# Last output tile in three column pieces, and 1/den spread to partitions by DMAs instead of matmuls

## The chip, the cores and the metric

The kernel runs on one core of a Trainium2 chip. The metric is device time in microseconds of one execution. Executions of one kernel mostly scatter by about 0.3 us either way.

## The reference, cut to what matters

```python
def _A_ref(x, wqkv, wo):                       # x: (1, 2048, 640), 32 heads of 20 features
    ...
    pq, pk = phi(q), phi(k)
    kv  = jnp.einsum("bhsd,bhse->bhde", pk, v)
    z   = jnp.einsum("bhsd->bhd", pk)
    num = jnp.einsum("bhqd,bhde->bhqe", pq, kv)
    den = jnp.einsum("bhqd,bhd->bhq", pq, z)[..., None] + 1e-6
    o = num / den
    return o.transpose(0, 2, 1, 3).reshape(B, S, D) @ wo

def _B_ref(x, w1, b1, w2, b2):                 # F = 1536
    return gelu(x @ w1 + b1) @ w2 + b2

return x + _A_ref(xn, ...) + _B_ref(xn, ...)   # xn = layernorm(x)
```

The kernel folds `kv` and `wo` into one matrix `Msb`. An output tile of 128 tokens is then one accumulation: 12 products of the MLP (`HG` with `W2`) and 5 of the attention (`PQ/den` with `Msb`). Dividing by `den` means scaling `PQ`, which has features on its partitions, by a row of 1/den for each head. `rden` has (chunk, head) on its partitions, so each head's row must be spread to the 4 partitions of that head in each of the 5 feature slices.

## The kernel before: the parts that the change touches

Tokens come in 4 chunks of 512 (`CW`), that is 16 tiles of 128. `HW` is 320, `JT` 12, `DT` 5, `H` 32. `E4` is the constant matrix of the matmul that copies each head's row to its partitions. `Pl.ins` records an instruction with the resources it reads and writes, and puts in the waits. Each engine runs its list in the order in which it was recorded.

```python
def rden_step(c, b):                       # spread 1/den of chunk c by a matmul, and scale PQ
    ...
    Pl.ins("tensor", lambda e: e.matmul(bank(b), E4[:, c, :], rden[:], start=True, stop=True), ...)
    Pl.ins("scalar", lambda e: e.activation(rs, bank(b), ACT.Copy), ...)
    for j in range(DT):                    # 5 DVE multiplications of 128x512
        Pl.ins(v, lambda e, j=j: e.tensor_tensor(out=PQ[:, j, cc], in0=PQ[:, j, cc], in1=rs, op=ALU.mult), ...)

def x_again(c):                            # reload of x for the residual, 640 KB, on SyncE
    Pl.ins("sync", ..., writes=[r_xr[c]] + r_xnT, dma=True)

def out_fin(t, b):                         # end of tile t
    s = t % 2                              # two output buffers only
    ...                                    # 10 matmuls PQ*Msb, 320 columns each
    xb(t)
    Pl.ins(v, ... out=halves(out_sb[:, s, :]), in0=pair(b), in1=halves(x_res[:, t, :]) ...)   # eviction
    Pl.ins("sync", lambda e: e.dma_start(ov[t * P:(t + 1) * P, :], out_sb[:, s, :]), ...)     # store

def out_last(t):                           # tile 15: two halves of 320 columns, each evicted and stored
    ...

bs = [out_w2(0)]
db = den_step()                            # den, then 1/den on DVE (rden)
bs += [out_w2(1), out_w2(2, 0, JT // 2)]
rden_step(0, db)
out_w2(2, JT // 2, JT, bs[2])
for t in range(3):
    out_fin(t, bs[t])
for t in range(3, NT - 1):
    b = out_w2(t)                          # 24 matmuls HG*W2
    if t in (3, 6, 10):
        rden_step({3: 1, 6: 2, 10: 3}[t], take(1))
    out_fin(t, b)
out_last(NT - 1)

for (waits, fns, ev, dma) in list(Pl.records["sync"]):   # SyncE waits for all its DMAs at the end
    if dma and ev is not None:
        Pl.wait_event("sync", ev)
```

The eviction of tile 2 writes the same buffer as tile 0, so it waits until the store of tile 0 has landed. The scaling of chunk 1 comes after that eviction in DVE's list.

## Time and profile before

| | before |
|---|---|
| device time, median of 6 runs | 212.06 us (211.77 to 212.39) |
| span in the trace | 210.7 us |
| TensorE busy | 205.5 us, 98% |
| first den matmul's start to last matmul's start | 72.57 us |
| last matmul's start to the end of the span | 3.15 us |

The page of the kernel before, its head (busy us, share of the span, instructions):

```profile
span 210.7 us, 3883 instructions
PE 205.5 (98%) x1585; PEld 140.1 (67%) x1585; DVE 110.5 (52%) x226; ACT 76.8 (36%) x145; POOL 20.5 (10%) x61
```

The chain of waits of the kernel before, in order of time (start us, us, what):

```profile
136.20 5.00 PE ps L600 x36
141.20 0.21 PE ps L570
141.41 8.96 PE ps L600 x66
150.38 0.22 PE ps L570
150.59 13.86 PE ps L600 x102
164.45 0.22 PE ps L570
164.67 18.47 PE ps L600 x136
183.14 0.22 PE ps L570
183.35 24.46 PE ps L600 x180
207.82 0.02 issue
207.84 0.49 DVE out_sb L632
```

L600 is an output matmul and L570 the E4 matmul that spreads 1/den. From 136 us on the chain is TensorE alone, without a gap: each E4 matmul pushes all later work back by 0.22 us. Only the last eviction (L632) and what follows it are not TensorE.

The timeline of the kernel before, 143 to 157 us, all engines, cut to the lines that matter (in brackets: idle before, and what ended it):

```profile
144.44 0.82 DVE L619 TENSOR_TENSOR out_sb<-ps,xnT 128x640 bf16<-128x640 f32 x1 [0.19 <-PE ps L600]
...
145.29 9.41 SPq L622 DMA_DIRECT2D out_dram<-out_sb  x4
...
149.76 0.82 DVE L619 TENSOR_TENSOR out_sb<-ps,xnT 128x640 bf16<-128x640 f32 x1 [2.74 <-DMA out_dram<-out_sb]
...
151.26 1.77 DVE L574 TENSOR_TENSOR PQ<-PQ,ek 128x512 bf16<-128x512 bf16 x5 [0.67 <-ACT ek L572]
...
155.05 1.52 PE L600 MATMUL ps<-Msb,PQ 128*128 128x320 bf16 x10
```

These are the evictions of tiles 0 and 2 (DVE, L619), the first stores on SyncE (SPq), the scaling of chunk 1 and TensorE's first use of it. The eviction of tile 2 already waits for a store (tile 0, issued at 145.29 and landed at 149.64). Nothing is lost by it: TensorE needs the scaled chunk only at 155.05.

SyncE's closing waits in the kernel before (count, ns, first and last start):

```profile
L108 SPq EVENT_SEMAPHORE  x17: 28/28/28, 208.7 to 210.2; - x17
```

The last store landed at 209.94, and the last of these waits ended at 210.23. The waits, not the landing, come last.

### The profile page before, as it was taken

Reading aid. Unit: us, or ns where it says so; the run is one execution under the profiler, and the core shown is the slowest. Engines: PE = TensorE matmul, PEld = TensorE weight load, DVE = VectorE, ACT = ScalarE, POOL = GpSimd, SP = SyncE. Lnnn points to the kernel's source line nnn. Section 1 sums busy time; section 2 is a strip of 40 time slices with the busy share of each in tenths; the row PEclk is TensorE's granted clock in tenths of the full one; section 3 lists DMA queues with packets and bytes.
Section 4 is the critical chain, followed back from the end, with each engine's and each line's share of the span. In section 5 each row is a group of like instructions: output and inputs, shape, how many; then the busy total and the mean of one; then the engine's idle time right before and its main releaser. Section 6 shows DMA issues by size and latency. Waiting matters only on the chain.

```text
span 210.7 us, 3883 instructions
## 1 busy us (share of the span) xinstructions
PE 205.5 (98%) x1585; PEld 140.1 (67%) x1585; DVE 110.5 (52%) x226; ACT 76.8 (36%) x145; POOL 20.5 (10%) x61
## 2 busy tenths in 40 slices
PE   7999999999999999999999999999999999999994
PEld 2689987444457777777666555677777777777772
DVE  4689981000008888999078866468451522263221
ACT  2579887666676554111253575110100100100000
POOL 2244557700000000000000000000000000000000
PEclk9999999999999999999999999999999999999999
DMA  5994758999000000000000000355411010001011
GB/s 165 340 349 99 101 111 101 347 321 346 10 0 0 0 3 0 0 3 0 0 0 3 0 5 0 124 138 170 163 35 54 9 65 31 31 31 34 31 62 33
DMA packets 21787, 17.46 MB, mean 83 GB/s; under 512 B 8713, under 2 KB 21769, under 8 KB 21769
## 3 DMA queue, kind: packets, MB, share of 16 engines
q1 hardware_dynamic: 21088, 16.72, 27.6%
q10 hardware_dynamic: 680, 0.49, 0.9%
q8 instruction: 12, 0.20, 0.4%
q14 instruction: 7, 0.05, 0.1%
HBM read 12.62 MB, written 2.62 MB: 72 GB/s over the span
## 4 chain that ended last, share of the span: by engine, by line
PE 86%; DVE 7%; DMA 4%; SPq 1%; issue 1%; DVEq 0%
PE ps L600 35%; PE ps L356 23%; PE ps L477 10%; PE ps L488 10%; PE ps L510 5%; DMA xPK<-in_A_x_dram 4%; DVE PQ L467 3%; DVE ek L465 1%; DVE W L534 1%; SPq L232 1%; PE ps L530 1%; PE ps L546 1%; DVE ZB L524 1%; PE ps L556 1%; DVE stats L313 0%
## 5 line engine op out<-in xcount | busy, mean ns | idle before, releaser
L600 PE MATMUL ps<-W,HG 128*128 128x320 bf16 x384 | 54.9, 299 | 0.0
L356 PE MATMUL ps<-xnT,W 128*128 128x128 bf16 (+2 forms) x435 | 52.0, 282 | 0.4 <-DMA W<-in_B_w_dram 0.4
L600 PEld LDWEIGHTS ps<-W,HG 128*128 128x128 bf16 x384 | 37.5, 98 | 15.2 <-issue 0.4
L356 PEld LDWEIGHTS ps<-xnT,W 128*128 128x128 bf16 x435 | 35.5, 98 | 16.1 <-DMA W<-in_B_w_dram 0.5
L360 ACT ACTIVATE HG<-ps,b1c 128x128 bf16<-128x128 f32 (+2 forms) x87 | 40.0, 492 | 13.2 <-PE ps L356 11.1
L465 DVE TENSOR_SCALAR ek<-ek 128x512 bf16<-128x512 bf16 (+1 forms) x36 | 10.9, 304 | 40.2 <-ACT ek L464 39.1
L464 ACT ACTIVATE ek<-ps 128x512 bf16<-128x512 f32 (+1 forms) x36 | 23.2, 644 | 20.4 <-PE ps L510 11.2
L619 DVE TENSOR_TENSOR out_sb<-ps,xnT 128x640 bf16<-128x640 f32 x15 | 12.4, 825 | 29.3 <-PE ps L600 26.2
L600 PE MATMUL ps<-Msb,PQ 128*128 128x320 bf16 x160 | 24.2, 299 | 0.0
L510 PE MATMUL ps<-xnT,Wqkv 128*128 128x512 bf16 x100 | 22.1, 379 | 0.0
L477 PE MATMUL ps<-Wqkv,xnT 128*128 128x320 bf16 x160 | 21.9, 299 | 0.0
L488 PE MATMUL ps<-xPK,xn_tm 128*128 128x320 bf16 x160 | 21.9, 299 | 0.0
L572 ACT ACTIVATE ek<-ps 128x512 bf16<-128x512 f32 x4 | 2.4, 597 | 49.2 <-PE ps L570 49.2
L600 PEld LDWEIGHTS ps<-Msb,PQ 128*128 128x128 bf16 x160 | 15.6, 98 | 6.3
L477 PEld LDWEIGHTS ps<-Wqkv,xnT 128*128 128x128 bf16 x160 | 15.7, 98 | 6.2
L488 PEld LDWEIGHTS ps<-xPK,xn_tm 128*128 128x128 bf16 x160 | 15.7, 98 | 6.1
L510 PEld LDWEIGHTS ps<-xnT,Wqkv 128*128 128x128 bf16 x100 | 11.6, 118 | 9.5 <-issue 0.2
L313 DVE BATCH_NORM_STATS2 stats<-xPK 128x6 f32<-128x320 bf16 x32 | 15.2, 475 | 3.5 <-DMA xPK<-in_A_x_dram 2.9
L467 DVE SCALAR_TENSOR_TENSOR PQ<-ps,ek 128x512 bf16<-128x512 f32 x20 | 13.8, 692 | 2.1
L467 DVE SCALAR_TENSOR_TENSOR xPK<-ps,ek 128x640 bf16<-128x640 f32 x16 | 13.2, 825 | 1.7
L498 DVE TENSOR_TENSOR Msb<-Msb,xPK 128x640 f32<-128x640 f32 x14 | 11.6, 825 | 0.5
L574 DVE TENSOR_TENSOR PQ<-PQ,ek 128x512 bf16<-128x512 bf16 x20 | 7.1, 419 | 9.0 <-ACT ek L572 9.0
(64 smaller groups left out, 89.3 us busy)
## 6 DMA issues: line engine op xcount, KB each, us to landing
xnT<-in_A_x_dram SPq DMA_DIRECT2D x4, 640.0 KB, 4.1
Wqkv<-in_A_wqkv_dram SPq DMA_DIRECT2D x3, 800.0 KB, 6.9
out_dram<-out_sb SPq DMA_DIRECT2D x15, 160.0 KB, 1.8
W<-in_B_w_dram SPq DMA_DIRECT2D x1, 1920.0 KB, 15.3
W<-in_B_w_dram SPq DMA_DIRECT2D x3, 480.0 KB, 7.6
xPK<-in_A_x_dram SPq DMA_DIRECT2D x2, 640.0 KB, 9.3
Wo<-in_A_wo_dram SPq DMA_DIRECT2D x1, 800.0 KB, 10.5
xPK<-in_A_x_dram SPq DMA_DIRECT2D x4, 160.0 KB, 4.5
```

What stands on the lines that cost most here:

```text
L313: Pl.ins(v, lambda e: e.bn_stats(stats[:, s, 6 * h:6 * h + 6], x_in[:, t, h * HW:(h + 1) * HW]), reads=[r_x[t]], writes=[r_stats[s]])
L356: Pl.ins("tensor", [(lambda e, k=k: e.matmul(bank(b, 0, w), W1[:, k, jb * P:(jb + 1) * P], xnT[:, k, tok], start=(k == 0), stop=(k == DT - ...
L360: Pl.ins("scalar", lambda e: e.activation(HG[:, jb, tok], bank(b, 0, w), ACT.Gelu_apprx_tanh, bias=b1c[:, jb:jb + 1]), reads=[B_[b], r_b1c ...
L464: Pl.ins("scalar", lambda e: e.activation(e2, src, ACT.Exp), reads=br, writes=[r_ek[s]])
L465: Pl.ins(v, lambda e: e.tensor_scalar(et, et, 1.0, 1e-6, ALU.min, ALU.add), reads=[r_ek[s]], writes=[r_ek[s]])
L467: Pl.ins(v, lambda e: e.scalar_tensor_tensor(out=d2, in0=src, scalar=0.0, in1=e2, op0=ALU.max, op1=ALU.add), reads=br + [r_ek[s]], writes= ...
L477: fns.append(lambda e, k=k, h=h, b=b, t=t: e.matmul(bank(b + h, 0, HW), xnT[:, k, t * P:(t + 1) * P], Wqkv[:, k, D + h * HW:D + (h + 1) * ...
L488: Pl.ins("tensor", [(lambda e, t=t, h=h, b=b, f=f: e.matmul(bank(b + h, 0, HW), xn_tm[:, t, f * P:(f + 1) * P], PK[:, t, h * HW:(h + 1) * ...
L498: Pl.ins(v, lambda e, t=t: e.tensor_tensor(out=zsum, in0=zsum, in1=PK[:, t, :], op=ALU.add), reads=[r_PK[t], r_zsum], writes=[r_zsum])
L510: Pl.ins("tensor", [(lambda e, k=k, j=j, b=b: e.matmul(bank(b), Wqkv[:, k, j:D:DT], xnT[:, k, cc], start=(k == 0), stop=(k == DT - 1))) fo ...
L600: return lambda e: e.matmul(bank(b + h, 0, HW), l, r[:, h * HW:(h + 1) * HW], start=(i == 0), stop=(i == JT + DT - 1))
L619: Pl.ins(v, lambda e: e.tensor_tensor(out=halves(out_sb[:, s, :]), in0=pair(b), in1=halves(x_res[:, t, :]), op=ALU.add), reads=B_[b:b + 2] ...
```

## The change

The intent is twofold. First, the last tile should end with a smaller piece, so that less eviction and store follow the last matmul. Second, three of the four E4 matmuls on the busy TensorE should be replaced by DMAs, on engines that are nearly idle.

```diff
+        def rden_dma(c):
+            for i in range(4):
+                Pl.ins("sync", lambda e, i=i: e.dma_start(rdb(c)[i:P:4, :], rden[H * c:H * (c + 1), :]),
+                       reads=[r_rden], writes=[r_rdb[c][i]] + ([r_rdb[0][i]] if c == 3 else []), dma=True)
...
         def out_last(t):
-            b = take(2)
             xb(t)
-            for h in range(2):
-                hs = slice(h * HW, (h + 1) * HW)
...
+            lo = 0
+            for i, w in enumerate((HW, 3 * 64, P)):
+                b = take(1)
...
         rden_step(0, db)
         out_w2(2, JT // 2, JT, bs[2])
+        for c in range(1, NC):
+            rden_dma(c)
         for t in range(3):
             out_fin(t, bs[t])
         for t in range(3, NT - 1):
             b = out_w2(t)
             if t in (3, 6, 10):
-                rden_step({3: 1, 6: 2, 10: 3}[t], take(1))
+                rden_scale({3: 1, 6: 2, 10: 3}[t])
             out_fin(t, b)
         out_last(NT - 1)
```

`rden_scale(c)` is the five DVE multiplications alone. Chunk 0 keeps its E4 matmul. The twelve DMAs stand on SyncE, ahead of the store of tile 0.

More of the change, by code (lines that the diff above doesn't have):

```diff
@@ L564, in den_step, with rden_scale, rdb @@
             return b
+        def rden_scale(c):
+            cc = slice(c * CW, (c + 1) * CW)
+            for j in range(DT):
+                Pl.ins(v, lambda e, j=j: e.tensor_tensor(out=PQ[:, j, cc], in0=PQ[:, j, cc], in1=rdb(c), op=ALU.mult),
+                       reads=r_rdb[c] + [r_PQ[c][j]], writes=[r_PQ[c][j]])
+        ekf = ek[:].rearrange("p a d -> p (a d)")
+        r_rdb = [[R_("rdb%d_%d" % (c, i)) for i in range(4)] for c in range(NC)]
+        def rdb(c):
+            return ekf[:, c % 3 * CW:(c % 3 + 1) * CW]
         def rden_step(c, b):
-            cc = slice(c * CW, (c + 1) * CW)
-            s = c % 3
-            rs = ek[:, s, 0:CW]
             Pl.ins("tensor", lambda e: e.matmul(bank(b), E4[:, c, :], rden[:], start=True, stop=True),
                    reads=[r_E4, r_rden], writes=[B_[b]])
-            Pl.ins("scalar", lambda e: e.activation(rs, bank(b), ACT.Copy), reads=[B_[b]], writes=[r_ek[s]])
-            for j in range(DT):
-                Pl.ins(v, lambda e, j=j: e.tensor_tensor(out=PQ[:, j, cc], in0=PQ[:, j, cc], in1=rs, op=ALU.mult),
-                       reads=[r_ek[s], r_PQ[c][j]], writes=[r_PQ[c][j]])
+            Pl.ins("scalar", lambda e: e.activation(rdb(c), bank(b), ACT.Copy), reads=[B_[b]],
+                   writes=r_rdb[c] + r_ek)
+            rden_scale(c)
+        def rden_dma(c):
+            for i in range(4):
+                Pl.ins("sync", lambda e, i=i: e.dma_start(rdb(c)[i:P:4, :], rden[H * c:H * (c + 1), :]),
+                       reads=[r_rden], writes=[r_rdb[c][i]] + ([r_rdb[0][i]] if c == 3 else []), dma=True)
         def x_again(c):
@@ L594, in bass_parallel_sum__linear_attn_block__dense_activation_gelu__prompt_kernel, with mm_ops @@
             x_again(c)
+        r_out3 = R_("out3")
+        def mm_ops(t, i):
+            tok = slice(t * P, (t + 1) * P)
+            return ((HG[:, i, tok], W2[:, i, :]) if i < JT else (PQ[:, i - JT, tok], Msb[:, i - JT, :]))
         def mm(b, t, i, h):
-            tok = slice(t * P, (t + 1) * P)
-            l, r = ((HG[:, i, tok], W2[:, i, :]) if i < JT else (PQ[:, i - JT, tok], Msb[:, i - JT, :]))
+            l, r = mm_ops(t, i)
             return lambda e: e.matmul(bank(b + h, 0, HW), l, r[:, h * HW:(h + 1) * HW],
@@ L625, in out_last @@
         def out_last(t):
-            b = take(2)
             xb(t)
-            for h in range(2):
-                hs = slice(h * HW, (h + 1) * HW)
-                Pl.ins("tensor", [mm(b, t, i, h) for i in range(JT + DT)],
-                       reads=[r for i in range(JT + DT) for r in mm_reads(t, i)], writes=[B_[b + h]])
-                Pl.ins(v, lambda e, h=h, hs=hs: e.tensor_tensor(
-                    out=out_sb[:, h, 0:HW], in0=bank(b + h, 0, HW), in1=x_res[:, t, hs], op=ALU.add),
-                    reads=[B_[b + h], r_xb[t]], writes=[r_out[h]])
-                Pl.ins("sync", lambda e, h=h, hs=hs: e.dma_start(ov[t * P:(t + 1) * P, hs], out_sb[:, h, 0:HW]),
-                       reads=[r_out[h]], dma=True)
+            lo = 0
+            for i, w in enumerate((HW, 3 * 64, P)):
+                b = take(1)
+                o = out_sb[:, (0, 1, 0)[i], (0, 0, HW)[i]:(0, 0, HW)[i] + w]
+                hs = slice(lo, lo + w)
+                lo += w
+                fns = []
+                for q in range(JT + DT):
+                    l, r = mm_ops(t, q)
+                    fns.append(lambda e, l=l, r=r, q=q, b=b, hs=hs, w=w: e.matmul(
+                        bank(b, 0, w), l, r[:, hs], start=(q == 0), stop=(q == JT + DT - 1)))
+                Pl.ins("tensor", fns, reads=[r for q in range(JT + DT) for r in mm_reads(t, q)], writes=[B_[b]])
+                Pl.ins(v, lambda e, b=b, hs=hs, w=w, o=o: e.tensor_tensor(
+                    out=o, in0=bank(b, 0, w), in1=x_res[:, t, hs], op=ALU.add),
+                    reads=[B_[b], r_xb[t]], writes=[r_out3 if i == 2 else r_out[i]])
+                Pl.ins("sync", lambda e, hs=hs, o=o: e.dma_start(ov[t * P:(t + 1) * P, hs], o),
+                       reads=[r_out3 if i == 2 else r_out[i]], dma=True)
         bs = [out_w2(0)]
```

## The prediction

> **What bounds the kernel now.** TensorE. Section 1 of the page: PE busy 205.5 of 210.7 us, clock 1.00. The chain of waits, in order of time, is unbroken PE work from 124.9 us to 207.8, then one DVE eviction (0.49). PE waits for nothing in the output stage. The median is 212.05 us.
>
> **Removed.** Three E4 matmuls of 512 columns (chunks 1 to 3). Each holds the chain for 0.22 us (pieces of the chain at 150.4, 164.5, 183.1), so 0.65 us in sum, all on the critical path. Three ACT copies of 0.60 us go too off the path; the DVE scalings (5 x 0.42 us a chunk) stay.
>
> **Last tile.** The second half, 17 matmuls of 320, becomes 17 of 192 and 17 of 128. The trace shows starts of 55.8 ns at 128 columns, 109.2 at 256, 135.8 at 320 and 215.8 at 512, each with its own weight load. That is the Trainium skill's N/2.4+2.5 (TensorE: Matmul & The Clock Gate, Back-to-back issue gap); the ~81 ns that the section gives for 128 columns beside weight loads does not show here. Estimate for 192: 82.5 ns. 17 x (82.5+55.8) = 2.35 us against 2.31: +0.04. The eviction on the chain shrinks: 320 columns 0.492, 640 columns 0.825, hence about 0.29 for 128: -0.20. The last store is issued 0.16 us earlier. The middle piece's eviction fits under the last 0.95 us of matmuls.
>
> **The end.** After the last store is issued (208.36, done 208.69), SyncE runs 17 semaphore waits, two semaphores each, from 208.74 to 210.23, about 0.065 us apart, with one hole of 0.48. The last store landed at 209.94, before these waits were through: the end is set by the waits, not by the landing. The change adds 12 DMAs in the spread and one more store, 13 more semaphores, so about 7 more waits: +0.42 us.
>
> **The spread.** The 12 DMAs (32 KB each, SBUF to SBUF) are issued on SyncE behind the x reload, whose fourth issue is at 144.36, and ahead of the first output store (now 145.29). Back-to-back issues took 0.40 to 0.55 us early in the trace, so about 5.5 us: the first store moves to about 150 and lands near 152. DVE's eviction of tile 2 waits for that (now it starts at 149.76), and chunk 1's scaling follows, 152.9 to 154.6. PE needs its first part at about 154.8 and the rest 0.27 us apart. Slack near 1.2 us: no stall expected, but it is the weak point[...]. Chunks 2 and 3 have ample time.
>
> **Sum.** 212.05 - 0.65 - 0.16 + 0.42 = 211.66; with some weight on a small PE stall, 211.7 us. Range 211.2 to 212.2. Faster by over 2%: 0.01; within 2%: 0.98; slower: 0.01.
>
> **What would show it.** Right: the chain of waits without E4 pieces; PE ending about 0.6 us earlier; starts of 82 and 56 ns in the last tile; last eviction near 0.29 us; about 24 closing waits on SyncE, taking near 1.9 us, ending after the last landing; DVE's idle before tile 2's eviction longer by 2 us, with no idle PE near 155. Wrong: PE idle between 150 and 156 with DVE scaling or a DMA as releaser; a last landing that ends after the waits.
>
> **What would make it wrong.** Longer issue of the 12 DMAs, stalling PE (+0.5 to 2 us); closing waits that cost less, or a second hole of 0.5; stores of 256-byte rows landing slowly.

## More of the kernel before

All runs used here are with a granted TensorE clock of 0.99 to 1.00.

The argument uses two things: ratios from interleaved runs, and distances in time inside the traces.

Absolute times of two traces should not be subtracted from one another.

## The result, and the profile after

The kernel after the change takes 212.36 us (median of 6 runs, 212.14 to 212.84) against 212.06 before. The ratio is 1.0017, with a 95% interval of 1.0003 to 1.0031. Here and below a ratio is the mean time of one kernel's fast runs over that of the other's in the same rounds, so it is not quite the ratio of the medians. The change makes the kernel about 0.3 us slower, where 0.35 us of gain was predicted.

| | before | after |
|---|---|---|
| first den matmul's start to last matmul's start | 72.57 us | 73.27 us |
| last matmul's start to the end of the span | 3.15 us | 2.82 us |
| store of tile 0 issued, landed | 145.29, 149.64 | 151.80, 153.84 |

The page after, its head:

```profile
span 210.4 us, 3928 instructions
PE 204.4 (97%) x1592; PEld 140.3 (67%) x1599; DVE 110.3 (52%) x227; ACT 75.1 (36%) x142; POOL 20.5 (10%) x61
```

The chain of waits after, in order of time:

```profile
155.12 0.01 DVE PQ L569
155.13 0.05 issue
155.18 47.97 PE ps L618 x350
203.15 4.67 PE ps L654 x51
207.83 0.02 issue
207.85 0.29 DVE out_sb L657
```

The E4 pieces are gone (the profile did not trace the chain back past 155 us), but at 155.12 there is something new. TensorE is no longer the head of its own chain: it was released by DVE's scaling of PQ (L569). At the end, the last eviction has shrunk from 0.49 to 0.29 us, as intended.

The timeline after, 143 to 157 us, all engines, cut to the lines that matter:

```profile
144.12 7.64 SPq L587 DMA_DIRECT2D ek<-rden  x12
...
151.80 3.35 SPq L640 DMA_DIRECT2D out_dram<-out_sb  x3
153.97 0.82 DVE L637 TENSOR_TENSOR out_sb<-ps,xnT 128x640 bf16<-128x640 f32 x1 [7.56 <-DMA out_dram<-out_sb]
154.71 1.76 DVE L569 TENSOR_TENSOR PQ<-PQ,ek 128x512 bf16<-128x512 bf16 x5
155.18 0.11 PEld L618 LDWEIGHTS ps<-Msb,PQ 128*128 128x128 bf16 x2 [1.13 <-DVE PQ L569]
155.18 1.79 PE L618 MATMUL ps<-Msb,PQ 128*128 128x320 bf16 x10 [0.80 <-DVE PQ L569]
155.51 0.11 PEld L618 LDWEIGHTS ps<-Msb,PQ 128*128 128x128 bf16 x2 [0.22 <-DVE PQ L569]
```

Read it from top to bottom. SyncE issues the twelve spread DMAs from 144.12 to 151.76, and only then the store of tile 0. That store lands at 153.84. The eviction of tile 2, which reuses the buffer, sat idle 7.56 us for it. The scaling of chunk 1 stands behind that eviction in DVE's list. TensorE, which would have been ready at about 154.2, waits for the scaling, and then follows it slice by slice: its 10 matmuls take 1.79 us in place of 1.52. Nothing in the chain waits for the DMAs' data: the rows for chunk 1 had landed by 149.06.

What the twelve DMAs cost SyncE (ns least/median/most, first and last start), and its closing waits, after:

```profile
L587 SPq DMA_DIRECT2D ek<-rden x12: 470/594/602, 144.1 to 151.2; - x12
```

```profile
L108 SPq EVENT_SEMAPHORE  x24: 17/28/28, 208.6 to 209.9; - x24
```

A median of 594 ns each, and about 0.64 us from one issue to the next. The 24 closing waits took no longer than the 17 before: the hole of 0.48 us does not appear among them.

### The profile page after: what moved, and what is told of

Its sections match the earlier page's. It is cut to its first block, busy times and chain, and to the rows that moved or that the text cites. A ratio compares the mean times of both kernels' runs of the same rounds, so it can differ in the third digit from the quotient of the medians.

```text
span 210.4 us, 3928 instructions
## 1 busy us (share of the span) xinstructions
PE 204.4 (97%) x1592; PEld 140.3 (67%) x1599; DVE 110.3 (52%) x227; ACT 75.1 (36%) x142; POOL 20.5 (10%) x61
## 5 line engine op out<-in xcount | busy, mean ns | idle before, releaser
L618 PE MATMUL ps<-W,HG 128*128 128x320 bf16 x360 | 51.4, 299 | 0.1
L618 PEld LDWEIGHTS ps<-W,HG 128*128 128x128 bf16 x360 | 35.1, 98 | 14.2 <-issue 0.4
L618 PE MATMUL ps<-Msb,PQ 128*128 128x320 bf16 x150 | 22.8, 299 | 0.8 <-DVE PQ L569 0.8
L510 PE MATMUL ps<-xnT,Wqkv 128*128 128x512 bf16 x97 | 21.4, 379 | 0.3 <-issue 0.2
L618 PEld LDWEIGHTS ps<-Msb,PQ 128*128 128x128 bf16 x150 | 14.2, 98 | 7.4 <-DVE PQ L569 2.0
L492 ACT ACTIVATE W<-ps 128x640 bf16<-128x640 f32 x5 | 3.5, 704 | 18.2 <-PE ps L488 14.6
L322 POOL TENSOR_TENSOR rstd<-veps,mhalf 128x1 f32<-128x1 f32 x16 | 9.2, 575 | 1.3
```

The lines of the kernel that those rows point to most:

```text
L510: Pl.ins("tensor", [(lambda e, k=k, j=j, b=b: e.matmul(bank(b), Wqkv[:, k, j:D:DT], xnT[:, k, cc], start=(k == 0), stop=(k == DT - 1))) fo ...
L618: return lambda e: e.matmul(bank(b + h, 0, HW), l, r[:, h * HW:(h + 1) * HW], start=(i == 0), stop=(i == JT + DT - 1))
```

## The experiments

All gave the right result, and each is compared with runs of the kernel before on the same chip (their medians: 212.13 us beside e1 to e4, 211.90 beside e5, e6, e7 and e9, 212.05 beside e10 and e11). "Stage" below is the time from the first den matmul's start to the last matmul's start in the trace, "end" that from there to the end of the span. The theory at the outset was the reading just given. The rivals were that the tail pieces cost the time, that the bytes of the spread come late or crowd the DMA engines, and that DVE simply has too little time there.

| run | median us | ratio to before (95%) | stage | end |
|---|---|---|---|---|
| before | 212.06 | 1 | 72.57 | 3.15 |
| the change | 212.36 | 1.0017 (1.0003 to 1.0031) | 73.27 | 2.82 |
| e1_tail_only | 211.95 | 0.9997 (0.9984 to 1.0010) | 72.69 | 2.91 |
| e2_spread_only | 212.81 | 1.0053 (1.0025 to 1.0081) | 73.16 | 3.04 |
| e3_scale_early | 211.36 | 0.9965 (0.9953 to 0.9977) | 72.04 | 2.81 |
| e4_act_queue | 211.23 | 0.9958 (0.9946 to 0.9970) | 72.04 | 2.91 |
| e5_three_dmas | 210.91 | 0.9949 (0.9934 to 0.9964) | 72.04 | 2.53 |
| e9_chunk3_later | 211.47 | 0.9980 (0.9955 to 1.0006) | 72.04 | 2.80 |
| e6_trim_before | 211.68 | 0.9980 (0.9967 to 0.9994) | 72.57 | 3.13 |
| e7_more_waits | 214.36 | 1.0111 (1.0093 to 1.0129) | 72.57 | 5.35 |
| e10_early_few_waits | 211.07 | 0.9947 (0.9935 to 0.9958) | 72.04 | 2.53 |
| e11_three_dmas_few_waits | 210.91 | 0.9946 (0.9932 to 0.9960) | 72.04 | 2.50 |

### e1_tail_only: the three pieces without the spread

The new `out_last` is put into the kernel before; the E4 matmuls stay.

> The kernel before with only the last tile in pieces of 320, 192 and 128; E4 matmuls kept. My theory (the tail pieces are a small gain, the loss is in the spread): last store issued about 0.2 us earlier, one closing wait more at most; 211.9 us beside 212.06, that is -0.05 to -0.4 us, no idle PE near 155 us. Rival (small pieces and 256-byte rows are what costs): 212.4 us or more, with the last landing later than 1.6 us after its issue.

The median is 211.95 us and the ratio 0.9997, not to be told from no change by time alone. The trace shows the expected small gain: the end shrinks by 0.24 us, while the stage grows by 0.12 (the last, shorter matmul starts later). There is no idle TensorE near 155 us, and the store of 256-byte rows landed 1.44 us after its issue, faster than the 1.58 of the 320-column store. The rival that the tail costs the time is out.

### e2_spread_only: the spread without the three pieces

The change with `out_last` of the kernel before.

> The change with the last tile of the kernel before. My theory: three E4 matmuls less (-0.65), a PE stall of about 1.2 us at tile 3's PQ matmuls near 155 us (+1.2), so 212.6 us. Rival (the tail pieces are what costs): -0.65 alone, 211.4 us.

It took 212.81 us, 0.2 above the expectation; two of its six runs, at 213.89 and 214.66 (the latter at a clock of 0.991), widen the interval, but all of it lies above 1. The loss is in the spread. The timeline of DVE in this kernel, 143 to 157 us:

```profile
154.66 0.82 DVE L637 TENSOR_TENSOR out_sb<-ps,xnT 128x640 bf16<-128x640 f32 x1 [7.58 <-DMA out_dram<-out_sb]
155.40 1.75 DVE L569 TENSOR_TENSOR PQ<-PQ,ek 128x512 bf16<-128x512 bf16 x5
```

It is the same wait of 7.6 us as in the change, and the same late scaling. The stage is 73.16 us; without three E4 matmuls it should be 72.57 - 0.65 = 71.92, so the stall costs 1.24 us.

### e3_scale_early: the scaling ahead of the eviction

```diff
         for t in range(3):
+            if t == 2:
+                rden_scale(1)
             out_fin(t, bs[t])
...
-            if t in (3, 6, 10):
-                rden_scale({3: 1, 6: 2, 10: 3}[t])
+            if t in (6, 10):
+                rden_scale({6: 2, 10: 3}[t])
```

> The change with chunk 1's scaling ahead of tile 2's eviction in DVE's order; the 12 DMAs and the late first store stay as they are. My theory (DVE's eviction of tile 2, waiting for the late first store, holds up the scaling that PE needs): scaling starts near 149 us, when its four DMAs have landed, tile 2's eviction still waits until about 154, PE stall gone, 211.2 us. Rival (the rows of 1/den themselves come late, or DVE is simply short of time there): the stall stays, 212.3 us.

The timeline of DVE, 143 to 157 us, in e3:

```profile
149.23 1.77 DVE L569 TENSOR_TENSOR PQ<-PQ,ek 128x512 bf16<-128x512 bf16 x5 [2.88 <-DMA ek<-rden]
150.91 0.48 DVE L596 TENSOR_TENSOR xnT<-xnT,b2bc 128x640 bf16<-128x640 bf16 x1
154.24 0.82 DVE L637 TENSOR_TENSOR out_sb<-ps,xnT 128x640 bf16<-128x640 f32 x1 [2.85 <-DMA out_dram<-out_sb]
```

The scaling starts at 149.23, as soon as the rows have landed, and is done by 151. Tile 2's eviction still waits until 154.24, as late as before, and it harms nothing. The stage drops from 73.27 to 72.04, by 1.23 us, and the ratio from 1.0017 to 0.9965. The twelve DMAs are all there, issued from 144.40 to 152.03 (144.12 to 151.76 in the change). So neither their data nor DVE's load held TensorE up; the order in DVE's list did, together with the late store. This is the strongest of the tests, because it changes the place of five instructions and nothing else. The time came 0.16 us above the expectation.

### e4_act_queue: the same DMAs from another queue

```diff
-                Pl.ins("sync", lambda e, i=i: e.dma_start(rdb(c)[i:P:4, :], rden[H * c:H * (c + 1), :]),
+                Pl.ins("scalar", lambda e, i=i: e.dma_start(rdb(c)[i:P:4, :], rden[H * c:H * (c + 1), :]),
```

> The change with the 12 DMAs issued by ACT instead of SyncE, same bytes; SyncE then also has 12 semaphores fewer to wait for at the end. My theory (what costs is SyncE's time to issue, 0.64 us each, ahead of the first store): first store issued near 145 us, tile 2's eviction near 150, no stall, about 210.9 us (0.25 of it from the closing waits). Rival (the 12 DMAs load the DMA engines or their descriptor generation, whoever issues them): the first store lands as late as in the change, the stall stays, 212.1 us.

The timeline of DVE, 143 to 157 us, in e4:

```profile
149.19 0.82 DVE L637 TENSOR_TENSOR out_sb<-ps,xnT 128x640 bf16<-128x640 f32 x1 [2.56 <-DMA out_dram<-out_sb]
149.93 1.76 DVE L569 TENSOR_TENSOR PQ<-PQ,ek 128x512 bf16<-128x512 bf16 x5
```

SyncE issued the first store at 144.89, it landed at 149.07, and the stall is gone although the same bytes move: the stage is 72.04. ACT could start the twelve 3 us sooner than SyncE in the change (141.06), as it has no reload of `x` ahead of them, so the bytes move somewhat earlier. Eight of the twelve still landed between 148.18 and 150.35, around the first store, which took 4.17 us to land where it took 4.35 in the kernel before. The rival that the DMA engines are crowded is out. ACT's issues took as long as SyncE's did (about 0.62 us each), but nothing that TensorE needs waits behind them on ACT. The expected 0.25 us from shorter closing waits did not come: 18 waits, but with the hole of 0.48 us among them again.

### e5_three_dmas: one DMA for each chunk

```diff
-            for i in range(4):
-                Pl.ins("sync", lambda e, i=i: e.dma_start(rdb(c)[i:P:4, :], rden[H * c:H * (c + 1), :]),
-                       reads=[r_rden], writes=[r_rdb[c][i]] + ([r_rdb[0][i]] if c == 3 else []), dma=True)
+            src = rden[H * c:H * (c + 1), :].unsqueeze(1).to_broadcast([H, 4, CW])
+            Pl.ins("sync", lambda e: e.dma_start(rdb(c), src),
+                   reads=[r_rden], writes=r_rdb[c] + (r_rdb[0] if c == 3 else []), dma=True)
```

> The change with each chunk's spread as one DMA of 128 rows (every source row read four times) instead of four of 32: 3 DMAs for 12, same bytes, still on SyncE ahead of the first store. My theory (SyncE pays 0.64 us for each DMA back to back, whatever its rows): about 1.9 us in all, first store near 146.5, no stall, and 9 semaphores fewer to wait for at the end; 211.1 us. Rival (the cost goes with rows or bytes, so one such DMA takes about 2.5 us): first store near 151, stall stays, 212.2 us.

What these DMAs cost SyncE in e5 (ns least/median/most, first and last start), and its DVE timeline, 143 to 157 us:

```profile
L587 SPq DMA_DIRECT2D ek<-rden x3: 544/593/674, 144.3 to 145.9; - x3
```

```profile
150.34 0.82 DVE L637 TENSOR_TENSOR out_sb<-ps,xnT 128x640 bf16<-128x640 f32 x1 [3.76 <-DMA out_dram<-out_sb]
151.08 1.75 DVE L569 TENSOR_TENSOR PQ<-PQ,ek 128x512 bf16<-128x512 bf16 x5
```

A DMA of 128 rows and 128 KB costs SyncE 593 ns, the same as one of 32 rows and 32 KB (594). Between these two shapes the cost is per DMA, not per row or byte. Three of them take 2.1 us, the first store is issued at 146.45, and the stall is gone. With nine semaphores fewer at the end, and no hole, the end is 2.53 us. At 210.91 us against 211.90 for the runs of the kernel before beside it, this beats both kernels.

### e9_chunk3_later: eight DMAs ahead of the store instead of twelve

```diff
-        for c in range(1, NC):
-            rden_dma(c)
+        rden_dma(1)
+        rden_dma(2)
         for t in range(3):
             out_fin(t, bs[t])
+        rden_dma(3)
```

> The change with chunk 3's four DMAs issued after the stores of tiles 0 to 2, so 8 of the 12 stand ahead of the first store. My theory: the first store moves up by 4 x 0.64 = 2.5 us to near 149.3, lands near 151.5, scaling of chunk 1 done its first part by 152.7, ahead of PE's need near 154.2: stall gone, 211.3 us. Rival (a DMA of the spread is slow whatever stands behind it): stall stays, 212.3 us.

The first store was issued at 149.89 and landed at 151.93. The timelines of DVE and then of TensorE in e9, 143 to 157 us:

```profile
152.06 0.82 DVE L637 TENSOR_TENSOR out_sb<-ps,xnT 128x640 bf16<-128x640 f32 x1 [4.97 <-DMA out_dram<-out_sb]
152.80 1.75 DVE L569 TENSOR_TENSOR PQ<-PQ,ek 128x512 bf16<-128x512 bf16 x5
```

```profile
151.64 3.42 PE L618 MATMUL ps<-W,HG 128*128 128x320 bf16 x24
154.90 1.52 PE L618 MATMUL ps<-Msb,PQ 128*128 128x320 bf16 x10
```

The scaling starts 2.1 us before TensorE's first use of it, and the 10 matmuls take their normal 1.52 us. The stall is a matter of threshold: four DMAs fewer in the way and it is nil. By time the run is less clear. One of its six executions took 213.05 us, at the lowest clock of the six (0.992, the others 1.00), and pulls the ratio to 0.998, with an interval that touches 1; the median of 211.47 and the stage of 72.04 agree with e3.

### e6_trim_before and e7_more_waits: the closing waits of the kernel before

e6 waits at the end for the last four stores alone. e7 appends 34 more semaphores, all of DMAs already waited for.

```diff
-        for (waits, fns, ev, dma) in list(Pl.records["sync"]):
-            if dma and ev is not None:
-                Pl.wait_event("sync", ev)
+        ends = [ev for (waits, fns, ev, dma) in Pl.records["sync"] if dma and ev is not None][-4:]
+        for ev in ends:
+            Pl.wait_event("sync", ev)
```

```diff
                 Pl.wait_event("sync", ev)
+        Pl.records["sync"].append(([("dma%d" % i, 16) for i in range(34)], [], None, False))
```

> The kernel before with closing waits on its last four stores alone (all other DMAs have been waited for by their users). My theory (the end is set by 17 closing waits, which finish 0.29 us after the last landing): two waits, the last ending about 0.1 us after the last landing, -0.2 us or a little more, 211.85 us. Rival (the landing of the last store sets the end): no change, 212.06 us.

> The kernel before with 34 more semaphores in the closing waits, all long passed: 17 more wait instructions. My theory (each such instruction costs 0.062 us at the end, as in the traces): +1.05 us, 213.1 us. Rival (they run in the shadow of the last landing): +0.75 us or less, or none.

SyncE's closing waits in e6, and in e7 (count, ns least/median/most, first and last start):

```profile
L108 SPq EVENT_SEMAPHORE  x2: 17/22/28, 208.4 to 209.7; - x2
```

```profile
L108 SPq EVENT_SEMAPHORE  x34: 28/28/1219, 208.4 to 212.0; - x34
```

e6 is inconclusive. Its waits did end 0.05 us after the last landing (209.64), yet its end is 3.13 us, no shorter than before. A gap of 0.45 us now lies between SyncE's last two instructions of the closing barrier, behind the waits; the other engines had passed that barrier by 210.04, SyncE only at 210.32. The measured ratio of 0.998 is a small gain that its trace does not account for.

e7 missed. It cost 2.4 us, not 1.05. In its trace the wait for the last store's semaphore was placed first (208.35, lasting 1.22 us until the landing), so the 33 others ran after the landing and none in its shadow. The cost of one is confirmed all the same: after the hole, 29 steps took 212.013 - 210.221 us, 0.062 us each.

The hole has a fixed place in SyncE's list: in all five traces that show it, it stands between the 79th and the 80th instruction that the trace records for SyncE. So it follows the fourth instruction after the last DMA in the kernel before and in e7; the third in e1 and e4, which have one more store ahead of it; and in e6 the fourth too, which is there the closing barrier's drain. In the change, e2, e3, e9 and e10, with 12 more DMAs on SyncE, and in e5 and e11 with 3 more, the 80th comes before the last store is issued, and no such hole appears after it. It is SyncE's, it goes with the count of instructions, and it costs time only where it falls after the last store. What makes it is not shown (the last point of this document says what is known).

### e10_early_few_waits and e11_three_dmas_few_waits

e3 and e5, each with closing waits on its last five stores alone. Here no hole was expected behind the landing.

> e3_scale_early with closing waits on the last five stores alone (the others have been waited for by their users). There 24 waits ended 0.32 us after the last landing, and no hole of 0.48 us stood in SyncE's stream near the end. My theory (closing waits at 0.062 us each delay the end where they outlast the landing): the last wait ends within 0.1 us of the last landing, so from the last matmul's start to the end 2.55 us instead of 2.81; about 0.25 us less than e3, 211.1 us. Rival (the landing sets the end, the waits run in its shadow): 2.8 us as in e3.

> e5_three_dmas with closing waits on the last five stores alone: the candidate for the best version. In e5 the waits ended 0.07 us after the last landing, so both theories expect next to nothing: 2.5 us from the last matmul's start to the end, 210.9 us. If the hole of 0.48 us in SyncE's stream falls behind the landing here, up to 0.45 us more.

SyncE's closing waits in e3, and in e10:

```profile
L108 SPq EVENT_SEMAPHORE  x24: 17/28/28, 207.7 to 209.1; - x24
```

```profile
L108 SPq EVENT_SEMAPHORE  x2: 28/28/28, 208.0 to 208.8; - x2
```

In e10 the end is 2.53 us against 2.81 in e3, as expected (2.55), and its median is 211.07 us. In the absence of the hole the closing waits are a real cost of 0.28 us. In e11 the end is 2.50 against 2.53 in e5, and the time 210.91 us, the same as e5: there was nothing left to take. e5, e10 and e11 are level at ratios of 0.9946 to 0.9949.

## Why the prediction was wrong

- **What bounds the kernel, and the E4 matmuls: right.** The three removed matmuls were priced at 0.65 us. From the stages, e1 to e3 is 72.69 - 72.04 = 0.65 us.
- **The last tile: right.** Predicted starts of 82 and 56 ns; in the trace after they are 82 to 83 and 55 to 56. Predicted eviction 0.29 us; measured 0.29. Predicted +0.04 us of matmuls; the chain has 4.67 us for the 51 matmuls, and 4.62 would be 34 of 320 columns.
- **The spread: the step that failed.** The prediction named this path in full: DMAs ahead of the first store, eviction of tile 2, scaling of chunk 1, TensorE. It then said "Back-to-back issues took 0.40 to 0.55 us early in the trace, so about 5.5 us" and "Slack near 1.2 us: no stall expected". The mechanism was right; the mis-sized term is SyncE's issue. The twelve took 151.80 - 144.12 = 7.68 us, 2.2 us more than 5.5, which exceeds the slack of 1.2 us by 1.0. Measured: TensorE's matmul starts are 1.10 us apart at 154.1 us where 0.14 is normal, so 0.96 us of waiting, and another 0.27 us while the 10 matmuls follow DVE's pace. Together that is the 1.23 us that e3 removed. The early issues were the wrong model: they were loads of other shapes, and the trace before had no DMAs of this shape back to back. It did hold a warning: at 35.09 us SyncE issued three loads of `Wqkv` in a row, which took 0.53 to 0.58 us each, with 0.57 to 0.63 from one issue to the next. Twelve at 0.6 us are 7.2, an estimate that already overruns the 5.5 by more than the slack.
- **The closing waits: wrong, by a cancellation.** "+0.42 us" for 7 more waits. Each does cost 0.062 us, but the waits' total went from 1.49 us to 1.42, because the hole of 0.48 us, which the prediction counted as part of them, no longer fell among them. A "second hole" was considered; that the first could move away was not.
- **The sum.** In the stage: -0.65 for E4, +0.12 for the later start of the last, shorter matmul, +1.23 for the stall, in all +0.70; measured +0.70. At the end: -0.20 for the eviction, -0.08 for the shorter last matmul (0.299 to 0.219 us), -0.07 for the closing waits, in all -0.35; measured -0.33. The two measured differences make +0.37 us, and the ratio of 1.0017 is +0.36 us of 212. Against the predicted -0.39, the stall is 1.23 too much and the closing waits 0.49 too little, so part of the first error was hidden by the second. That was luck: the prediction did not know that the hole would move.

The Trainium skill helps to place this. On who issues, "DMA: Bandwidth & Descriptors", section "Issuing engines are not separate DMA queues", says that issuing from several engines only saves the sequencer's time, "usually small relative to the DMA itself". e4 agrees with the first half: the sequencer's time was what moving the DMAs to ACT saved. The second is no comfort here: one issue (0.59 us) was a third of the 1.8 us that the quickest of these DMAs took to land, but twelve in a row held SyncE for 7.64 us, and that is what made the first store late. "Perfetto Trace Analysis", section "DMA Optimizations", suggests balancing over engines where an issuing engine looks busy with slices; SyncE's 7.64 us of issues with hardly a gap is that picture. And the advice in the DMA page's "Rules for kernel authors" to coalesce small transfers, with mostly overhead under 64 KB, holds in e5: 3 of 128 KB cost SyncE 2.1 us, about a quarter of the 7.64 for 12 of 32 KB.

## What to carry to other kernels

Work that is moved from a full engine to an idle one still takes a place in some engine's ordered list; ask what stands behind it there, and follow that wait through the buffers it holds until it comes back to the full engine. When a plan's slack is about as large as the uncertainty of one of its durations, take the safe order at once: here the scaling ahead of the eviction, another queue, or one DMA in place of four each removed the stall and turned +0.3 us into -0.8 to -1.0 (the stage is 72.04 in all three; they differ in the end). Look at what follows the last store, too: waits for things long done cost time there one by one.

## What the Trainium skill lacked or had wrong

- "TensorE: Matmul & The Clock Gate", "Back-to-back issue gap", gives about 81 ns a matmul at 128 columns and 131 at 512 for streams of weight loads and matmuls, and N/2.4+2.5 as the isolated gap. In streams, each matmul with its own weight load, the starts are about 56 ns apart at 128 columns, 82 to 83 at 192, 136 at 320 and 216 at 512: the formula throughout.
- "DMA: Bandwidth & Descriptors", "Issuing engines are not separate DMA queues", calls the issue time usually small beside the DMA. Issued back to back, SBUF to SBUF, a DMA held SyncE 0.59 us, for 32 rows as for 128, and landed 1.8 to 4.4 us after its issue; the next began about 0.64 us after it at 32 rows, 0.72 and 0.83 at 128; a lone store held it 0.33 us, the store right behind the twelve 0.58. I found no figure for this pitch in the pages.
- No page that I found prices closing semaphore waits on SyncE: 0.062 us for each instruction of two semaphores, up to 0.28 us behind the last landing (e3 against e10).
- No page that I found gives a time for the hole of about 0.48 us at a fixed place in SyncE's list (before, e1, e4, e6, e7). The nearest is "Runtime: NRT & Kernel Launch", "Instruction fetch mechanics": an engine's instructions are refilled in blocks, and the cost of crossing a block's end is called mostly hidden. "CRC Debugging", "Comparing the Two Runs", names queue 14 as the one that refills instructions. In those five traces the last packet of that queue starts between 208.8 and 211.0 us, and in all others by 204.5. It starts 0.62 to 0.65 us after the hole. In all twelve traces it follows the start of SyncE's 79th recorded instruction, by 1.08 to 1.12 us where that is a wait and by 1.40 to 1.67 where it is a store. So hole and refill go with the same place in SyncE's list; that crossing it makes the hole is not tested.
